# GpSimd makes the clamps of two of seventeen weight pieces; ranks and loads are renumbered

## The chip, the cores and the metric

The kernel runs on one core of a Trainium2 chip. The core has a matrix engine (TensorE, PE in the rows; its weight loads are PEld), a vector engine (VectorE, DVE), an activation engine (ScalarE, ACT), a general engine (GpSimd, POOL) and an engine that issues transfers (SyncE, SP; its queue is SPq). Each works off its own list of instructions in order; semaphores hold an instruction until what it needs is there. The metric is the device time of one execution in microseconds.

## The reference

One attention with product features, followed by a mixer of two small networks, for batches of 4, a sequence of 1088 and a width of 128 (4 heads of 32):

```python
def phi(x):
    a = np.einsum('rd,bhsd->bhsr', S1, x)
    b = np.einsum('rd,bhsd->bhsr', S2, x)
    return np.einsum('bhsi,bhsj->bhsij', a, b).reshape(*x.shape[:-1], r * r)
q_p, k_p = (phi(q), phi(k))
kv = np.einsum('bhsf,bhsd->bhfd', k_p, v)
z = np.sum(k_p, axis=2)
x = num / den            # num = q_p kv, den = q_p z + 1e-06, laid out (B, S, 128)
h = np.maximum(xt @ w_tok1, 0.0) @ w_tok2     # xt: x with S and channels swapped
u = x + h.transpose(0, 2, 1)
h2 = np.maximum(u @ w_ch1, 0.0) @ w_ch2       # 128 -> 1536 -> 128
return (u + h2).astype(np.float32)
```

The four weight matrices come in as 64-bit floats.

## The kernel before

**Weights.** The four matrices (0 to 3: wt1, wt2, wc1, wc2) are cut into seventeen pieces, `w00` to `w32` (matrix, then piece), 256 to 512 columns of 128 partitions. `LOADS` is the order in which SP loads the pieces, and with them the keys, queries and values of batches 0 and 1 (`k0`, `q0a`, `q0b`, `v0`, `k1`, `q1`, `v1`). A 64-bit piece (`doubles`) becomes 32-bit by a chain in `convert` (L373 to L416): `abs` (ACT, L384, tile `c`) and `low` (ACT, L388, tile `tail`), then `clamp` (L391), `shift` (L395, into a PSUM bank) and `merge` (L398), all three on DVE, then `add` (POOL, L405 into `whole`, or L407 in place). Pieces of matrices 2 and 3 at once, and those of 0 and 1 later, are split into a high half (`hi`, ACT, L504) and the remainder (`lo`, POOL, L507), tile `halves`. Batch 0 is mixed with `whole` pieces, everything else with halves.

**Stages of a batch b.** `K` projects keys (L534), copies half of them (ACT, L544), multiplies (DVE, L564, tile `k_p`) and sums with the values (PE, L581); ACT copies the result as `kvz` (L591). `Q` makes the query features: for batch 0 on PE (L672) with copies by ACT (L690, L694, tile `xT`) and products on DVE (L700) or POOL (L697); for the others by row writes and reads through memory (L744 to L760) and products on POOL (L770). `A` is the attention (PE, L790), the division (DVE, L806, L808), the token network (L846 or L852, L886, L968 or L972) and, for batch 0, transposes of x (`u0` to `u2`, L877). `U` is the channel network over spans of 384 columns of all batches: a first-layer group of three matmuls on PE (L1022, into one of three PSUM banks `ps_h`), ACT's `hh` (L1026) and DVE's `hl` (L1029), which frees that bank, and a second-layer group of three matmuls (L1035).

**What sets the order.** The program's order is made on the host by a list planner, `Plan.run` (L222). Each operation has a table of engines with costs (`ways`), what it waits for (`after`, `takes`) and a rank: the length of the chain behind it plus a number of its own from `LEAD`. The planner steps through a clock of its own and issues the ready operation of the highest rank. Operations with `port=True` on DVE, and all of POOL, reserve a common `port` in it. Where PE would idle it puts in filler matmuls (`fill`, L362). What it emits is each engine's list, in order; the chip then only waits for semaphores. A buffer of which there are few (`bufs`: four `c`, four `tail`, three `ps_a`, three `ps_h`) is reused in that order.

Of the kernel before, what the change touches and what calls it, by code (L numbers as in the profile page):

```python
# [65 lines left out]

LEAD = {
    "A0.d1": -168600.0,
    "A0.d2": -1620100.0,
    "A0.t2": -90600.0,  # L70
    "A0.u0": -461300.0,
    "A0.u1": 126500.0,
    "A0.ul00": 26500.0,
    "A1.n1": 207400.0,
    "A1.xT0": -108100.0,
    "A2.h0": -154900.0,
    "A2.n0": 210600.0,
    "A2.w1": -3726400.0,
    "A2.w2": -80800.0,
    "A2.x": -16100.0,  # L80
    "A2.xb": -788400.0,
    "A3.n0": 775400.0,
    "A3.n1": 210300.0,
    "A3.w1": 89200.0,
    "A3.w2": 127600.0,
    "K0.kvz": -2428600.0,
    "K1.c0": 982200.0,
    "K1.kvz": -2006700.0,
    "K1.s": -439400.0,
    "K1.v0": 26700.0,  # L90
    "K1.v4": -1229500.0,
    "K2.p": 5500.0,
    "K2.s": 631300.0,
    "K3.p": 645000.0,
    "Q0.a20": 606400.0,
    "Q0.m20": -56700.0,
    "Q0.p1": 183300.0,
    "Q1.r00": 75800.0,
    "Q1.r01": 221700.0,
    "Q1.r11": -287800.0,  # L100
    "Q3.p": -1564300.0,
    "U0.l": -3600.0,
    "U0.s": -888200.0,
    "U1.ol": 570300.0,
    "U1.s": -310000.0,
    "U10.s": -2000.0,
    "U11.s": -1400.0,
    "U2.f": 181200.0,
    "U2.h": -146700.0,
    "U2.s": -764700.0,  # L110
    "U3.f": 8400.0,
    "U3.s": 5700.0,
    "U4.f": 762600.0,
    "U4.h": 68000.0,
    "U6.s": -230900.0,
    "U8.f": 192500.0,
    "U8.s": -591000.0,
    "U9.f": -390200.0,
    "U9.h": 261700.0,
    "s.low": 6600.0,  # L120
    "s.rows": 95400.0,
    "w00.clamp": -462300.0,
    "w00.lo": -3161100.0,
    "w01.abs": 311700.0,
    "w01.hi": -124600.0,
    "w01.lo": -2636700.0,
    "w02.abs": 28200.0,
    "w02.hi": -455000.0,
    "w02.lo": -4313300.0,
    "w02.low": -1051800.0,  # L130
    "w02.shift": 141200.0,
# [1 line left out]
    "w03.hi": -107500.0,
    "w03.lo": -2645500.0,
    "w03.shift": -1556200.0,
    "w04.hi": -2453000.0,
    "w04.lo": -2852800.0,
    "w10.abs": -1284500.0,
# [1008 lines left out]
```

## Time and profile before

| | us |
|---|---|
| median of 3 runs (220.74 to 222.49) | 220.97 |
| the profiled execution | 220.62 |
| its span, first to last instruction | 218.70 |
| PE busy | 211.2 |
| DVE busy | 137.7 |
| ACT busy | 117.3 |
| POOL busy | 80.3 |

The rows further down are from the profiled execution; times count from the start of its span. A row of the timeline has the start, the duration, the engine, the line, the operation with output and inputs, and in brackets the time for which the engine idled before it and what released it. `x2` after a row means that neighbouring instructions were merged; their durations overlap a little, since an engine begins an instruction before the write of the one before has been acknowledged. Work on engines other than PE costs time only where PE waits for it.

### The profile page before, as it was taken

The numbers are of one execution on the slowest core, as the hardware profiler recorded it, in microseconds if no ns is written. First come the engines' busy times: TensorE is split into PE (matmuls) and PEld (weight loads), VectorE is DVE, ScalarE is ACT, GpSimd is POOL, SyncE is SP. The second block draws the span as 40 slices with busy tenths as digits, with TensorE's granted clock in tenths as the row PEclk, the third lists the DMA queues.
The fourth block names the chain that finished last, engine by engine and source line by source line (L and its number), as shares of the span: only waits on it lengthen the run. The fifth ranks groups of instructions, "written<-read, shape, count | busy, mean of one in ns | idle before, by whom it ended". The sixth has DMA issues, their size and how long they took to land.

```text
span 218.7 us, 4927 instructions
## 1 busy us (share of the span) xinstructions
PE 211.2 (97%) x1884; PEld 199.4 (91%) x1884; DVE 137.7 (63%) x276; ACT 117.3 (54%) x283; POOL 80.3 (37%) x87
## 2 busy tenths in 40 slices
PE   7997999998999999999999999999999999999994
PEld 7766679997998999999999999999999999999993
DVE  2887999879759456555833455568137655556562
ACT  4588799994545324543532544455226544355551
POOL 3165597989899102740500220745003200000000
PEclk9999999999999999999999999999999999999998
DMA  6999996994106589610250258400510000100000
GB/s 194 390 410 407 406 393 205 186 211 151 37 3 226 128 223 155 172 66 3 85 170 0 74 142 146 174 0 27 191 38 1 3 36 0 36 3 36 0 30 27
DMA packets 11399, 28.36 MB, mean 130 GB/s; under 512 B 1520, under 2 KB 5616, under 8 KB 11376
## 3 DMA queue, kind: packets, MB, share of 16 engines
q1 hardware_dynamic: 11232, 27.79, 41.3%
q8 instruction: 15, 0.25, 0.5%
q10 hardware_dynamic: 144, 0.26, 0.4%
q14 instruction: 8, 0.07, 0.1%
HBM read 23.21 MB, written 4.83 MB: 128 GB/s over the span
## 4 chain that ended last, share of the span: by engine, by line
PE 83%; DMA 11%; DVE 1%; SPq 1%; issue 1%; ACT 0%
PE ps_h L1022 33%; PE ps_o L1035 32%; DMA doubles<-wt 11%; PE ps_a L852 4%; PE ps_a L972 4%; PE ps_a L790 3%; PE ps_a L581 3%; PE ps_a L968 1%; PE ps_a L534 1%; SPq L366 1%; PE ps_a L727 1%; DVE k_p L564 1%; PE ps_a L877 0%; PE ps_a L886 0%; DVE hl L1029 0%
## 5 line engine op out<-in xcount | busy, mean ns | idle before, releaser
L1029 DVE SCALAR_TENSOR_TENSOR hl<-ps_h,hh 128x384 fp32r<-128x384 f32 (+2 forms) x144 | 74.9, 532 | 54.9 <-ACT hh L1026 54.5
L1026 ACT ACTIVATE hh<-ps_h 128x384 fp32r<-128x384 f32 (+2 forms) x144 | 67.8, 477 | 58.7 <-PE ps_o L1035 36.2
L1022 PE MATMUL ps_h<-uh,halves 128*128 128x384 f32 (+2 forms) x288 | 88.1, 334 | 0.9 <-DVE hl L1029 0.9
L1035 PE MATMUL ps_o<-hh,halves 128*128 128x384 f32 (+2 forms) x288 | 70.6, 327 | 0.0
L1022 PEld LDWEIGHTS ps_h<-uh,halves 128*128 128x128 f32 x288 | 53.3, 188 | 4.0 <-DVE hl L1029 2.7
L1035 PEld LDWEIGHTS ps_o<-hh,halves 128*128 128x128 f32 x288 | 50.3, 188 | 0.0
L1022 PE MATMUL ps_h<-ul,halves 128*128 128x384 f32 (+2 forms) x144 | 47.0, 327 | 0.0
L1035 PE MATMUL ps_o<-hl,halves 128*128 128x384 f32 (+2 forms) x144 | 47.0, 327 | 0.0
L1022 PEld LDWEIGHTS ps_h<-ul,halves 128*128 128x128 f32 x144 | 27.1, 188 | 0.2
L1035 PEld LDWEIGHTS ps_o<-hl,halves 128*128 128x128 f32 x144 | 27.0, 188 | 0.0
L946 POOL TENSOR_TENSOR ul<-us,uh 128x64 fp32r<-128x64 f32 (+4 forms) x15 | 9.6, 656 | 46.5 <-ACT uh L943 46.3
L770 POOL TENSOR_TENSOR qp<-qp,br 128x544 f32<-128x544 f32 x12 | 16.2, 1367 | 13.2 <-PE ps_o L1035 9.7
L818 POOL TENSOR_TENSOR xl<-x,xh 128x384 fp32r<-128x384 f32 x9 | 8.9, 1014 | 13.5 <-ACT xh L814 8.5
L564 DVE TENSOR_TENSOR k_p<-ps_a,a_sb 128x1024 f32<-128x1024 f32 (+1 forms) x12 | 11.0, 948 | 4.3 <-ACT a_sb L544 4.3
L405 POOL TENSOR_TENSOR whole<-c,tail 128x512 int32<-128x512 int32 (+3 forms) x11 | 11.7, 1071 | 3.3 <-ACT abT L736 2.0
L384 ACT ACTIVATE c<-doubles 128x512 f32<-128x512 f32 (+3 forms) x17 | 10.7, 628 | 3.2 <-DMA doubles<-wt 2.2
L507 POOL TENSOR_TENSOR halves<-whole,halves 128x384 fp32r<-128x384 f32 (+3 forms) x11 | 11.5, 1062 | 0.0
L790 PEld LDWEIGHTS ps_a<-kvz,qp 128*64 128x64 f32 x288 | 8.8, 138 | 2.5 <-ACT kvz L591 1.3
L790 PE MATMUL ps_a<-kvz,qp 128*64 128x66 f32 x288 | 9.5, 224 | 1.4 <-ACT kvz L591 1.1
L388 ACT ACTIVATE tail<-doubles 128x512 int32<-128x512 uint32 (+3 forms) x17 | 10.5, 624 | 0.0
L395 DVE TENSOR_SCALAR ps_h<-c 128x512 int32<-128x512 int32 (+3 forms) x17 | 10.3, 617 | 0.1
L398 DVE SCALAR_TENSOR_TENSOR c<-doubles,ps_h 128x512 int32<-128x512 int32 (+3 forms) x17 | 10.3, 609 | 0.1
(78 smaller groups left out, 229.0 us busy)
## 6 DMA issues: line engine op xcount, KB each, us to landing
qp<-rows SPq DMA_DIRECT2D x6, 544.0 KB
br<-rows SPq DMA_DIRECT2D x12, 272.0 KB
doubles<-wc SPq DMA_DIRECT2D x6, 512.0 KB
v_sb<-v SPq DMA_DIRECT2D x4, 594.0 KB
doubles<-wt SPq DMA_DIRECT2D x4, 512.0 KB
k_sb<-kT SPq DMA_DIRECT2D x3, 576.0 KB
xm<-xb SPq DMA_DIRECT2D x3, 576.0 KB
xT<-xm SPq DMA_DIRECT2D x12, 144.0 KB
```

The source lines that it names most:

```text
L384: nc.scalar.activation(f32(t["c"]), f32(high), AF.Abs)
L388: nc.scalar.activation(t["tail"], low.bitcast(U32), AF.Copy, scale=2.0 ** -29)
L395: nc.vector.tensor_scalar(t["ps"], t["c"], 3, 0x3FFFFFFF, op0=ALU.logical_shift_left, op1=ALU.bitwise_and)
L405: engines[e].tensor_tensor(dst(), t["c"], t["tail"], op=ALU.add)
L507: engines[e].tensor_tensor(halves[w, i][:, 1], f32(whole[w, i] if w < 2 else t["c"]), f32(halves[w, i][:, 0]), op=ALU.subtract)
L564: engines["pool" if on_pool else "dve"].tensor_tensor(t["k_p"][:pn, t0 * H:t1 * H], a.unsqueeze(3).broadcast_to([pn, n, R, R]), t["sb", t0 ...
L770: engines[e].tensor_tensor(qp[:, p, cs], qp[:, p, cs], t["br"][:, p, cs], op=ALU.mult)
L790: nc.tensor.matmul(x_ps[c:c + 64, o:o + 2 * (D + 1)], lhsT=qp[:, p, s0 + c:s0 + c + 64], rhs=kvz_all[b % 2][:, p, :2 * (D + 1)], start=Tru ...
L1022: nc.tensor.matmul(h_ps[:, :cn], lhsT=part(2, at[2][e][0], l, at[2][e][1] * P, P), rhs=r[:, :cn], start=(m == 0), stop=(m == 2))
L1026: nc.scalar.activation(t["hh"][:, :cn], t["h"][:, :cn], AF.Relu)
L1029: nc.vector.scalar_tensor_tensor(t["hl"][:, :cn], t["h"][:, :cn], 0.0, f32(t["hh"][:, :cn]), op0=ALU.max, op1=ALU.subtract)
L1035: nc.tensor.matmul(outs[i][:, :cn], lhsT=part(3, at[3][e][0], l, at[3][e][1] * P, P), rhs=r[:, :cn], start=(e == 0 and m == 0), stop=(e == ...
```

## The change

Two pieces, `w03` and `w15`, have their `clamp` on POOL. The new set `CLAMPS_ON_POOL` names them, and the planner is given a cost for that (141 + 1.6 per column, in its own ns). `LEAD` is exchanged as a whole (95 entries against 102), and `LOADS` is put in another order; nothing else is touched. `m.alt` is read by nothing in the kernel.

```diff
-LOADS = "k0 q0a 00 v0 q0b 01 02 03 04 10 k1 11 12 13 q1 20 32 30 21 v1 31 15 22 14".split()
+LOADS = "00 q0a q0b v0 k0 02 01 03 04 10 k1 q1 12 13 11 20 30 32 31 22 21 14 15 v1".split()
+CLAMPS_ON_POOL = {"w03", "w15"}
 LEAD = {
...
-    "w03.clamp": 120200.0,
-    "w15.clamp": 149200.0,
...
+    "w14.clamp": 147200.0,
...
-        def clamp(_):
-            nc.vector.tensor_scalar(f32(t["c"]), f32(t["c"]), LEAST, MOST, op0=ALU.max, op1=ALU.min)
+        def clamp(e):
+            engines[e].tensor_scalar(f32(t["c"]), f32(t["c"]), LEAST, MOST, op0=ALU.max, op1=ALU.min)
...
-        m = plan.add(name + ".clamp", dve2(n), clamp, [a], (), [c_hold], port=True)
+        m = plan.add(name + ".clamp", {"pool": 141 + 1.6 * n} if name in CLAMPS_ON_POOL else dve2(n), clamp, [a], (), [c_hold], port=True)
+        if not keep:
+            m.alt = [{"pool": 141 + 1.6 * n}]
```

The lists of the engines are new everywhere, though mostly by neighbours that swap. Three places follow. Pieces appear in them as `doubles_` with a running number; the line numbers of the changed kernel are 7 to 9 higher.

ACT, from the abs of w02 (before) and of w01 (now) to the first key sums' copy `kvz` and the copies `xT` of the last queries of batch 0. Before (`doubles_91` is w03, `_92` w04, `_93` w10, `_90` w02):

```order
L384 ACTIVATE c<-doubles_91 128x512
L388 ACTIVATE tail<-doubles_91 128x512
L384 ACTIVATE c<-doubles_92 128x256
L388 ACTIVATE tail<-doubles_92 128x256
L388 ACTIVATE tail<-doubles_93 128x384
L591 COPY kvz_82<-ps_o 64x2x33 x2
L690 COPY xT<-ps_a 128x320
L694 COPY xT<-ps_h 128x320
L690 COPY xT<-ps_a 128x320
L388 ACTIVATE tail<-doubles_90 128x512
L798 ACTIVATE den<-ps_a 128x12
```

Now (`_91` is w03, `_90` w01, `_92` w04, `_93` w10):

```order
L391 ACTIVATE c<-doubles_91 128x512
L395 ACTIVATE tail<-doubles_90 128x512
L391 ACTIVATE c<-doubles_92 128x256
L600 COPY kvz_82<-ps_o 64x2x33 x2
L395 ACTIVATE tail<-doubles_92 128x256
L699 COPY xT<-ps_a 128x320
L703 COPY xT<-ps_h 128x320
L699 COPY xT<-ps_a 128x320
L807 ACTIVATE den<-ps_a 128x12
L395 ACTIVATE tail<-doubles_93 128x384
```

The copy of `kvz` stands behind one tail after the abs of w03 instead of three.

DVE, in the channel network, around the clamps of w14 and w15. Before (`_98` is w32, `_104` w14; the two clamps of 320 columns are w15's and w14's, and fifteen `hl` stand ahead of them in all):

```order
L398 SCALAR_TENSOR_TENSOR c<-doubles_98,ps_h 128x512
L1029 SCALAR_TENSOR_TENSOR hl<-ps_h,hh 128x384 x3
L391 TENSOR_SCALAR c<-c 128x320 x2
L1029 SCALAR_TENSOR_TENSOR hl<-ps_h,hh 128x384 x2
L395 TENSOR_SCALAR ps_h<-c 128x320
L1029 SCALAR_TENSOR_TENSOR hl<-ps_h,hh 128x384
L398 SCALAR_TENSOR_TENSOR c<-doubles_104,ps_h 128x320
L395 TENSOR_SCALAR ps_h<-c 128x320
```

Now (`_99` is w32, `_104` w15, `_103` w14; the clamp is w14's, and seventeen `hl` stand ahead of it):

```order
L405 SCALAR_TENSOR_TENSOR c<-doubles_99,ps_h 128x512
L1038 SCALAR_TENSOR_TENSOR hl<-ps_h,hh 128x384
L402 TENSOR_SCALAR ps_h<-c 128x320
L1038 SCALAR_TENSOR_TENSOR hl<-ps_h,hh 128x384
L405 SCALAR_TENSOR_TENSOR c<-doubles_104,ps_h 128x320
L1038 SCALAR_TENSOR_TENSOR hl<-ps_h,hh 128x384 x4
L398 TENSOR_SCALAR c<-c 128x320
L1038 SCALAR_TENSOR_TENSOR hl<-ps_h,hh 128x384
L402 TENSOR_SCALAR ps_h<-c 128x320
L405 SCALAR_TENSOR_TENSOR c<-doubles_103,ps_h 128x320
```

One clamp has left DVE, the other stands alone and further back, and the shift of w15 stands three `hl` earlier than a shift of 320 columns did.

POOL, from the split of w31 to the last two query products of batch 1 (`qp`). Before (`halves_698` is w31, `_759` w22, `_836` w32, `whole_892` and `_904` w15 and w14; the split of w21 stands just ahead):

```order
L507 TENSOR_TENSOR halves_698<-c,halves_698 128x512
L407 TENSOR_TENSOR c<-c,tail 128x512
L507 TENSOR_TENSOR halves_644<-whole_515,halves_644 128x384
L507 TENSOR_TENSOR halves_759<-c,halves_759 128x512
L770 TENSOR_TENSOR qp<-qp,br 128x544
L407 TENSOR_TENSOR c<-c,tail 128x512
L770 TENSOR_TENSOR qp<-qp,br 128x544
L507 TENSOR_TENSOR halves_836<-c,halves_836 128x512
L1051 TENSOR_TENSOR o_sb<-uh,ul 128x384
L507 TENSOR_TENSOR halves_717<-whole_481,halves_717 128x384
L405 TENSOR_TENSOR whole_892<-c,tail 128x320
L405 TENSOR_TENSOR whole_904<-c,tail 128x320
```

(then the last two products). Now (`halves_713` is w31, `_786` w22, `_836` w32; the splits of w21 and of a 384-wide piece stand just ahead):

```order
L516 TENSOR_TENSOR halves_713<-c,halves_713 128x512
L414 TENSOR_TENSOR c<-c,tail 128x512
L516 TENSOR_TENSOR halves_721<-whole_406,halves_721 128x384
L398 TENSOR_SCALAR c<-c 128x320
L516 TENSOR_TENSOR halves_786<-c,halves_786 128x512
L414 TENSOR_TENSOR c<-c,tail 128x512
L779 TENSOR_TENSOR qp<-qp,br 128x544
L516 TENSOR_TENSOR halves_836<-c,halves_836 128x512
L779 TENSOR_TENSOR qp<-qp,br 128x544
L412 TENSOR_TENSOR whole_884<-c,tail 128x320
L412 TENSOR_TENSOR whole_896<-c,tail 128x320
L516 TENSOR_TENSOR halves_899<-whole_884,halves_899 128x320
```

(then the last two products). The clamp of w15 stands between two splits, the split of w22 behind a further 384-wide one, and one query product has gone behind the split of w32.

## Rows read from the trace of the kernel before

**Rows 1.** the page: busy time of PE, share of the span, instructions

```profile
PE 211.2 (97%) x1884; PEld 199.4 (91%) x1884; DVE 137.7 (63%) x276; ACT 117.3 (54%) x283; POOL 80.3 (37%) x87
```

**Rows 2.** busy by stretch: us, PE, PEld, DVE, ACT, POOL, PEclk, DMA share, GB/s

```profile
60.00:70.00 10.00, 10.00 (x155) 9.15 (x160) 7.48 (x15) 4.92 (x16) 10.00 (x11) 1.00 0.25 81
```

**Rows 3.** waits of PE: line, waited for, total us, times, longest

```profile
PE ps_a L790 <- ACT kvz L591: 1.1, 1, 1.1
```

**Rows 4.** timeline of ACT in the head, around the copy of kvz

```profile
14.72 0.69 ACT L384 ACTIVATE c<-doubles 128x512 f32<-128x512 f32 x1 [0.70 <-DMA doubles<-wt]
15.31 0.67 ACT L388 ACTIVATE tail<-doubles 128x512 int32<-128x512 uint32 x1
15.88 0.41 ACT L384 ACTIVATE c<-doubles 128x256 f32<-128x256 f32 x1
16.21 0.85 ACT L388 ACTIVATE tail<-doubles 128x256 int32<-128x256 uint32 x2
16.96 0.42 ACT L591 COPY kvz<-ps_o 64x66 f32<-64x66 f32 x2
17.41 0.43 ACT L690 COPY xT<-ps_a 128x320 f32<-128x320 f32 x1
```

**Rows 5.** timelines of DVE and PE in the head

```profile
18.27 1.02 DVE L395 TENSOR_SCALAR ps_h<-c 128x256 int32<-128x256 int32 x2
29.18 1.22 DVE L564 TENSOR_TENSOR k_p<-ps_a,a_sb 128x1024 f32<-128x1024 f32 x1
...
30.45 0.55 PE L877 MATMUL ps_a<-ident,x 128*128 128x128 f32 x3 [0.15 <-DVE k_p L564]
...
34.11 2.32 PE L581 MATMUL ps_a<-v_sb,k_p 128*64 128x66 f32 x72
```

**Rows 6.** timeline of SP's queue, issues (start, duration)

```profile
29.05 0.30 SPq L744 DMA_DIRECT2D rows<-abT  x1
30.32 0.30 SPq L744 DMA_DIRECT2D rows<-abT  x1
31.19 0.35 SPq L366 DMA_DIRECT2D k_sb<-kT  x1
```

**Rows 7.** timelines of DVE, POOL and PE around 51 us; one group of clamps

```profile
51.29 1.41 DVE L391 TENSOR_SCALAR c<-c 128x320 f32<-128x320 f32 x1
51.14 1.37 POOL L507 TENSOR_TENSOR halves<-c,halves 128x512 fp32r<-128x512 f32 x1
53.22 0.44 PE L1022 MATMUL ps_h<-uh,halves 128*128 128x384 f32 x1 [0.90 <-DVE hl L1029]
...
L391 DVE TENSOR_SCALAR c<-c 128x384 f32<-128x384 f32 x4 | 1.3, 352 | 0.0
```

**Rows 8.** POOL by form: count, busy us, mean ns, idle before; one timeline row

```profile
L770 POOL TENSOR_TENSOR qp<-qp,br 128x544 f32<-128x544 f32 x12 | 16.2, 1367 | 13.2 <-PE ps_o L1035 9.7 <-DMA br<-rows 3.3 <-POOL ul L946 0.2
L507 POOL TENSOR_TENSOR halves<-c,halves 128x512 fp32r<-128x512 f32 x6 | 8.0, 1340 | 1.5 <-ACT halves L504 1.5
L507 POOL TENSOR_TENSOR halves<-whole,halves 128x384 fp32r<-128x384 f32 x4 | 4.1, 1022 | 0.0
L405 POOL TENSOR_TENSOR whole<-c,tail 128x320 int32<-128x320 int32 x2 | 1.8, 878 | 0.9 <-DVE c L398 0.9
L654 POOL COPY s_spread<-s_blocks 128x256 f32<-128x256 f32 x1 | 0.4, 398 | 2.7 <-DVE s_blocks L403 2.7
L697 POOL TENSOR_TENSOR qp<-xT 128x384 f32<-128x384 f32 x2 | 2.0, 1005 | 6.4 <-ACT xT L690 6.4
...
40.35 2.74 POOL L507 TENSOR_TENSOR halves<-c,halves 128x512 fp32r<-128x512 f32 x2
```

**Rows 9.** timelines of DVE and PE: twelfth hl, first use of w22, attention

```profile
47.28 0.55 DVE L1029 SCALAR_TENSOR_TENSOR hl<-ps_h,hh 128x384 fp32r<-128x384 f32 x1
...
49.03 0.34 PE L1022 MATMUL ps_h<-uh,halves 128*128 128x384 f32 x1
60.65 2.32 PE L790 MATMUL ps_a<-kvz,qp 128*64 128x66 f32 x72
```

More of the change, by code (lines that the diff above doesn't have):

```diff
@@ L65 @@
 KEYS_ON_POOL = set()
+CLAMPS_ON_POOL = {"w03", "w15"}
 LEAD = {
[L68 to L131, printed above, removed]
-    "w03.clamp": 120200.0,
[L133 to L138, printed above, removed]
-    "w10.clamp": 69000.0,
-    "w11.clamp": 246000.0,
-    "w11.hi": -1243300.0,
-    "w11.lo": -134000.0,
-    "w11.low": 448400.0,
-    "w11.merge": -659300.0,
-    "w12.abs": 99900.0,
-    "w12.hi": 475400.0,
@@ L147 @@
-    "w12.low": -24500.0,
-    "w12.merge": -269500.0,
-    "w13.hi": -300400.0,
-    "w13.merge": -144100.0,
-    "w13.shift": -1219700.0,
-    "w14.abs": -2780200.0,
-    "w14.clamp": 192400.0,
-    "w15.abs": -4153500.0,
-    "w15.clamp": 149200.0,
-    "w20.clamp": -574900.0,
-    "w20.low": -1570500.0,
-    "w21.low": 310000.0,
-    "w22.abs": -997600.0,
-    "w22.low": -1298000.0,
-    "w32.abs": -2006300.0,
-    "w32.low": -2863700.0,
+    "A0.d0": -120600.0,
+    "A0.d1": -804800.0,
+    "A0.d2": -1067500.0,
@@ new lines @@
+    "K1.kvz": -1115600.0,
+    "K1.v4": -253500.0,
+    "K2.c0": -235200.0,
+    "K3.p": 764300.0,
+    "K3.s": -896200.0,
+    "Q0.a00": -139800.0,
+    "Q0.a11": 171500.0,
+    "Q0.a20": 586400.0,
+    "Q0.b11": 321100.0,
+    "Q0.p2": -471600.0,
+    "Q1.m00": 189000.0,
+    "Q1.r01": -156700.0,
+    "Q2.p": -401200.0,
+    "Q3.p": -3203400.0,
+    "U0.l": -388200.0,
+    "U0.oh": -343700.0,
+    "U0.s": -489000.0,
+    "U1.s": -2281100.0,
+    "U10.s": -13800.0,
+    "U11.f": -12400.0,
+    "U11.s": -13600.0,
@@ new lines @@
+    "U2.f": -129800.0,
+    "U2.l": -1302400.0,
+    "U2.s": -61100.0,
+    "U3.f": 42700.0,
+    "U4.f": 374000.0,
+    "U4.s": -215500.0,
+    "U5.s": -23800.0,
+    "U6.s": -122100.0,
+    "U7.f": -191700.0,
+    "U7.h": 106300.0,
+    "U7.s": -555000.0,
+    "U8.s": 149000.0,
+    "s.low": 118500.0,
+    "v3": -527800.0,
+    "w00.lo": -3021100.0,
+    "w00.low": 25600.0,
+    "w01.clamp": 96800.0,
+    "w01.hi": -78200.0,
+    "w01.lo": -5573600.0,
+    "w01.low": -177200.0,
+    "w02.lo": -4693900.0,
@@ new lines @@
+    "w03.hi": -155900.0,
+    "w03.lo": -2709800.0,
+    "w03.low": -892100.0,
+    "w04.abs": 215400.0,
+    "w04.clamp": 413100.0,
+    "w04.hi": -1905800.0,
+    "w04.lo": -457000.0,
+    "w04.merge": -398500.0,
+    "w10.abs": -554900.0,
+    "w10.hi": -457500.0,
+    "w10.low": -157100.0,
+    "w12.hi": 30700.0,
+    "w12.merge": -24100.0,
+    "w13.hi": 986800.0,
+    "w13.low": -366600.0,
+    "w13.shift": -540600.0,
+    "w14.abs": -680700.0,
+    "w14.clamp": 147200.0,
+    "w14.lo": -487000.0,
@@ L163 @@
+    "w14.low": 28600.0,
+    "w15.abs": -3843300.0,
+    "w15.shift": 198500.0,
+    "w20.hi": 754000.0,
+    "w20.low": 270500.0,
+    "w22.abs": -73100.0,
+    "w22.low": 70900.0,
+    "w30.low": -524000.0,
+    "w30.shift": -98400.0,
+    "w31.abs": 122900.0,
+    "w31.hi": -378000.0,
+    "w32.abs": -581300.0,
+    "w32.clamp": 184400.0,
+    "w32.lo": 51700.0,
+    "w32.low": -2668600.0,
 }
```

21 lines of the change are left out of this document (added).

## The prediction

> **What bounds the kernel now.** I read the page's busy shares first: TensorE (PE) is busy for 211.2 of 218.7 us [rows 1]. No other engine comes near, so the time is PE's own work plus the moments in which PE has nothing to do. The busy time by stretch says where those lie: from 60 us on PE is full, as in the stretch shown (10.00 of 10.00) [rows 2]. So there are two places to look at: the head, up to about 34 us, in which the weights are converted and batch 0 is mixed, and any hole after it. In the body the change adds no matmul and drops none, and in the head it drops only four filler matmuls, which are the planner's stop-gaps for idle time. Its effect is therefore how much earlier the body starts, plus the holes that close, less the holes that open. PE's waits name two that the change can touch: 1.1 us in the head for the copy of `kvz` by ACT (L591) [rows 3], and one hole of 0.90 us in the body, for an `hl` of DVE (L1029) [rows 7].
>
> **The change, term by term.**
>
> *Head: the copy of kvz.* The head is anchored where piece w03 lands: ACT waits for it and starts at 14.72 [rows 4]. Its landing should not move. Eight loads stand in the queue up to and with 03, before (k0 q0a 00 v0 q0b 01 02 03) and now (00 q0a q0b v0 k0 02 01 03): the same eight. Before, ACT did w03's abs and tail, w04's abs, then two tails (w04, w10), and the copy of kvz at 16.96, the q copies from 17.41. Now, by the order, come w03's abs, w01's tail (as wide as w03's), w04's abs, and kvz; w10's tail goes behind. With the spacings of the rows (0.59, 0.57, 0.33) kvz starts at 14.72 + 1.49 = 16.21. It takes 0.45 (16.96 to 17.41), w04's tail alone some 0.33 (the spacing of its equally wide abs), and the q copies start at 16.99: **0.42 us earlier**.
>
> Does that reach the body? The work behind these copies on DVE is the same pieces in the same places, only with other piece numbers, up to the key product of batch 1 (29.18), which PE waits for at 30.45 [rows 5]. The clamp of w03 leaves DVE, but from a place where DVE waited for ACT anyway, so I count nothing for it. So u1 starts at 30.03, and the value sums of batch 1 (L581), at 34.11 before, want to start at 33.69. These need the values v1, and v1 is now the last of the weights' loads (slot 25 of SP's queue) instead of slot 21. SP issues each load as an older one lands: the issues at 29.05, 30.32 and 31.19 are spaced 1.27 for a 512 KB piece and 0.87 for a 320 KB one [rows 6]. Eight issues lie between an issue and the landing that allows it, so 31.19 is the landing of slot 23. Two loads were left behind it, 512 and 320 KB, so the stream of equal bytes ends at 31.19 + 1.27 + 0.87 = 33.33. That is 0.36 us before v1 is needed. Cost 0, but the cover is thin.
>
> *The hole.* Before, the clamps of w15 and w14 stand together on DVE in front of the sixteenth `hl`. The second takes 1.41 us, where a wider one takes 0.352 in the mean, because GpSimd (POOL) runs a split from 51.14 to 52.51 and the clamp gets through only at its end [rows 7]. The `hl` behind it is late, its PSUM bank with it, and the next first-layer group on PE starts at 53.22 after 0.90 us of idling [rows 7]. Now w15's clamp is POOL's, and w14's stands alone, two `hl` later. It can still be held by a POOL instruction, but look at what waits behind it: the eighteenth `hl`, then the 21st first-layer group, which takes over that bank. Between the 18th group and the 21st, PE's order has two more groups of the first layer and four of the second. A group is three matmuls, 0.52 us as the body's rows are spaced. So PE has 6 x 0.52 = 3.1 us of work there, against one POOL instruction of at most 1.37 [rows 8], the clamp itself (0.35), and one `hl` (0.55). Term: **0.90 us** gained.
>
> Here the Trainium skill speaks against the change. SBUF — State Buffer, "Who interferes with whom", says that GpSimd and a DVE instruction in a 2-port mode take the pair of ports whole, that the one that issues first blocks the other, and that issue order decides; the clamp held for 1.41 us agrees. Read strictly, a clamp on POOL holds the port as a clamp on DVE waits for it, and the hole would only move: the sum would then be 0.42 alone. I go by the order above, in which the wait has cover.
>
> *What POOL pays.* POOL gets two instructions that no row of before shows: a clamp, one input, 128x512 and 128x320. Bounds for 320: from below the one-input copy of 128x256 scaled, 0.398 x 320/256 = 0.50; from above the two-input add, 0.878 [rows 8]. I take 0.6, near the copy, which has one input as well. The w03 clamp runs while POOL waits for q copies: free. The w15 clamp stands in a queue that PE follows closely, so I add it up. Before, the splits of w21 and w31 start at 40.35 [rows 8]; less 0.42 that is 39.93. Then, by the order, two 512 splits and one 384, one 512 add (a split's price), one 384 split, the clamp: 3 x 1.34 + 2 x 1.02 + 0.6 = 6.66, to 46.6. The split of w22 ends at 47.9. PE's row at 49.03 is the first that uses w22 [rows 9]; less 0.42, and two matmuls of 0.17 further for the low half, that is 48.96: in time by 1.0. After it come a 512 add, a product of 544, w32's split, a product, two 320 adds, a 320 split and two products: 47.9 + 2 x 1.34 + 4 x 1.37 + 3 x 0.88 = 58.7. The next attention of PE, at 60.65 before [rows 9], comes at 60.65 - 0.42 - 0.90 = 59.3. In time by 0.6; at the upper price of a clamp by 0.3. Cost 0, bounds 0 and about 0.5 if durations add up without their overlaps.
>
> DVE gets a new wait, the shift of w15 for POOL's clamp. Behind it are further `hl`. POOL's clamp ends at 46.6; DVE comes to this shift after its twelfth `hl`, the one that ran from 47.28 to 47.83 before [rows 9], so to 47.4 now. In time by 0.8.
>
> *Sum.* 0.42 + 0.90 = 1.32. The profiled execution took 220.62 us, of which the span is 218.70 and 1.92 lie around it; 218.70 - 1.32 + 1.92 = **219.3**. The median of the three runs shown, 220.97, is 0.35 above that execution; I predict against the execution. Behind 60 us PE is full, so nothing more is won there, and the tail is the same four groups.
>
> **Rivals.**
> *The likeliest, 219.3:* both terms hold. Its own range is 218.8 to 219.9. Chance 0.45.
> *The hole moves instead of closing, 220.2:* w14's clamp, POOL's clamp of w15 or the attention that waits for POOL's last product costs a wait of the same size; only 0.42 is kept. For it: covers of 0.3 to 0.9 us in a queue that I added up over twenty instructions. Against: the cover of w14's clamp is over 3 us of PE work. Chance 0.26.
> *More than the two terms, 218.6:* the value sums end at 34.11 + 2.32 = 36.4 [rows 5], and to the group at 49.03 PE does 23 groups of 0.52 in 12.6 us, which by themselves are 12.0; so about 0.65 us is lost there in small waits, and another order could close them all: 219.3 - 0.65 = 218.65. For it: these follow a DVE that clamps hold up. Against: no single wait of PE above 0.3 us is named there. Chance 0.14.
> *v1 comes late, up to 221.1, slower than before:* the value sums wait for v1, and PE stands in order behind them. Each us past 33.69 costs one us; from 35.0 on (33.69 + 1.32) the kernel is slower than before. The latest that the stream could end is 35.5, if the row writes mix in; 219.3 + 1.8 = 221.1. For it: a cover of only 0.36. Against: the bytes ahead of v1 are those that had landed at 33.33 before. Chance 0.09.
> *POOL's first clamp pays for loading its code, 219.3 + (x - 2.8):* POOL has never run this operation before w03. w03's abs is ready at 15.4 (14.72 and 0.69 [rows 4]). DVE's shift of w03 is the second of two at 18.27, so it started at about 18.6 before [rows 5], and 0.42 earlier is 18.2. A price x up to 2.8 is free; above that everything in DVE's queue is late, and from x = 4.1 on the kernel is slower than before. Against it: POOL's first two-input product costs no more than the next (mean 1005 ns over both) [rows 8], so x should be near 0. Chance 0.06. GPSIMD Engine Reference of the Trainium skill, "2.1 Instruction dispatch", gives about 6 us for the first call to a freshly loaded kernel; by that figure the time would be an estimated 222.5, and nothing in this trace shows such a load.
>
> **How the numbers follow.** A change of 1% is about what a measurement of this kernel can tell from none; from 220.97 that is 218.8 and 223.2. Faster by over 1% is the third case and a little of the first's lower edge: 0.15. Slower by over 1% needs the code load or something I have not seen: 0.08. The rest, 0.77, is within 1%. The range must leave out two in ten: 218.4 takes in the third case, 221.2 the late v1.
>
> **What would show it.** Right: the copy of kvz starts near 16.2 and the first value sums of batch 1 near 33.7; PE's waits no longer have 0.9 us for `hl`; POOL's 128x320 clamp takes 0.5 to 0.9; the attention stands near 59.3. Wrong: the copy of kvz not earlier, which would mean that w03 landed later; a wait of the value sums (L581) for the load of v1; a wait of DVE's shift for POOL; a wait of the attention for POOL's product; or a first POOL clamp of several us.

## The result, and the profile after

The changed kernel takes 218.28 us (median of six runs, 218.02 to 218.36) against 220.86 us for the kernel before beside it: a ratio of 0.9869, 95% interval 0.9839 to 0.9899. It is 1.3% faster. Two later sets of runs of the same file, each beside the kernel before on another chip, gave 0.9912 (0.9887 to 0.9937; 218.59 us) and 0.9897 (0.9874 to 0.9921; 218.48 us). The forecast was 219.3 us with a range from 218.4: the sign was right, and the forecast gain (1.32 us from the profiled execution) was about half of the measured one (2.40). The first set lies just below the range, the two later sets inside it. One run of a later kernel (220.84 us, w03's clamp alone on POOL) was over 1.5% above that kernel's fastest run and is left out of its figures.

| | before | after | difference |
|---|---|---|---|
| profiled execution, us | 220.62 | 218.22 | -2.40 |
| its span, us | 218.7 | 216.3 | -2.4 |
| copy of kvz by ACT starts | 16.96 | 15.68 | -1.28 |
| value sums of batch 1 on PE start | 34.11 | 33.28 | -0.83 |
| attention of batch 1 on PE starts | 60.65 | 58.80 | -1.85 |

After the change each line number of the kernel is 7 to 9 higher than in the rows of before. The page's busy time of PE (us, share of the span, instructions) against [rows 1]:

```profile
PE 209.9 (97%) x1876; PEld 198.7 (92%) x1876; DVE 136.7 (63%) x274; ACT 117.4 (54%) x284; POOL 83.1 (38%) x88
```

PE's busy time is 1.3 us shorter: four fillers are gone (38 of their records against 46), and some losses that count as busy (below). The waits of PE (line, waited for, total us, times, longest):

```profile
PE ps_o L369 <- POOL ident masks.py:199: 1.4, 1, 1.4
PE ps_a L799 <- ACT kvz L600: 0.4, 1, 0.4
PE ps_a L855 <- DVE x L817: 0.3, 1, 0.3
PE ps_a L895 <- ACT h L873: 0.3, 1, 0.3
PE ps_a L886 <- DVE k_p L573: 0.2, 1, 0.2
```

The 0.9 us for `hl` [rows 7] is gone, and the wait for the copy of `kvz` fell from 1.1 [rows 3] to 0.4. Where the copy comes from, in ACT's timeline (start, duration, line, out<-in), against [rows 4]:

```profile
13.33 0.49 ACT L699 COPY xT<-ps_a 128x384 f32<-128x384 f32 x1
13.69 0.72 ACT L391 ACTIVATE c<-doubles 128x512 f32<-128x512 f32 x1
14.27 0.71 ACT L395 ACTIVATE tail<-doubles 128x512 int32<-128x512 uint32 x1
15.34 0.44 ACT L391 ACTIVATE c<-doubles 128x256 f32<-128x256 f32 x1 [0.36 <-DMA doubles<-wt]
15.68 0.42 ACT L600 COPY kvz<-ps_o 64x66 f32<-64x66 f32 x2
```

w03's abs starts at 13.69, directly behind a copy: the load was there. Before, ACT had stood idle for it until 14.72. Now ACT waits 0.36 us for the next load, w04. POOL's two clamps and DVE's, from the timelines of POOL and DVE:

```profile
15.58 1.91 POOL L398 TENSOR_SCALAR c<-c 128x512 f32<-128x512 f32 x1
45.75 1.28 POOL L398 TENSOR_SCALAR c<-c 128x320 f32<-128x320 f32 x1
50.81 1.30 POOL L516 TENSOR_TENSOR halves<-c,halves 128x512 fp32r<-128x512 f32 x1
...
47.06 0.49 DVE L402 TENSOR_SCALAR ps_h<-c 128x320 int32<-128x320 int32 x1 [0.32 <-POOL c L398]
51.56 0.74 DVE L398 TENSOR_SCALAR c<-c 128x320 f32<-128x320 f32 x1
```

POOL's clamp is dearer than its sum of two inputs of the same width (0.878 for 128x320 in [rows 8]), and DVE's shift of w15 waits 0.32 us for it. w14's clamp on DVE (51.56) is held until POOL's split has ended, 0.74 instead of some 0.3, and no wait of PE follows.

**Where the 2.40 us are.** 0.83 are in the head. The hole of before costs more than its wait says. PE's timeline of before around it; between these rows stands the one at 53.22 in [rows 7]:

```profile
51.98 0.34 PE L1035 MATMUL ps_o<-hl,halves 128*128 128x384 f32 x1
...
53.50 0.34 PE L1022 MATMUL ps_h<-ul,halves 128*128 128x384 f32 x1
```

From 51.98 to 53.22 are 1.24 us where the rows of the body are 0.17 apart, and from 53.22 to 53.50 are 0.28: the hole costs 1.07 + 0.11 = 1.18 us, not 0.90. The wait is counted from the modelled end of the last matmul, 0.34 after its start. Two smaller losses went too, behind the point from which I had called PE full. In before, the query projection of a later batch (L727) stands by itself among the channel network's matmuls; after, value sums and keys follow it directly. PE's timelines of before and then of after at this place:

```profile
69.50 0.31 PE L1035 MATMUL ps_o<-hl,halves 128*128 128x320 f32 x1
69.74 0.69 PE L727 MATMUL ps_a<-q_sb,s_rows 64*32 64x272 f32 x16
70.36 0.41 PE L1022 MATMUL ps_h<-uh,halves 128*128 128x320 f32 x1
70.61 0.31 PE L1022 MATMUL ps_h<-ul,halves 128*128 128x320 f32 x1
```

```profile
68.69 0.69 PE L736 MATMUL ps_a<-q_sb,s_rows 64*32 64x272 f32 x16
69.34 2.32 PE L590 MATMUL ps_a<-v_sb,k_p 128*64 128x66 f32 x72
71.47 1.24 PE L543 MATMUL ps_a<-s_blocks,k_sb 128*64 128x64 f32 x36
```

Rows of one kind are 0.15 apart there; from the last row of the channel network to the projection it is 0.24, and from the first row after it to the next 0.25, so an excursion costs about 0.2. PE's order goes over between matmuls on `halves` and others 25 times before and 23 times after: one excursion fewer. And one pair of matmuls at 89.67 of before lasts 0.78 instead of 0.51, a stall of 0.28 us that after does not have. 0.83 + 1.18 + 0.2 + 0.28 = 2.5, against 2.40 measured. The part behind the attention is not one execution's chance: from the start of the attention of batch 1 to the start of the last matmul PE takes 154.55 us before and 153.93 after; it is 154.5 to 154.7 in the five other profiles with the order of before (the kernel planned anew aside), and 153.9 to 154.2 in the eleven others with the order of after.

### The profile page after: what moved, and what is told of

It reads as the page before. It is cut to its first block, busy times and chain, and to the rows that moved or that the text cites. A ratio compares the mean times of both kernels' runs of the same rounds, so it can differ in the third digit from the quotient of the medians.

```text
span 216.3 us, 4917 instructions
## 1 busy us (share of the span) xinstructions
PE 209.9 (97%) x1876; PEld 198.7 (92%) x1876; DVE 136.7 (63%) x274; ACT 117.4 (54%) x284; POOL 83.1 (38%) x88
## 4 chain that ended last, share of the span: by engine, by line
PE 79%; DVE 5%; ACT 5%; DMA 4%; SPq 2%; issue 2%; POOL 1%; DVEq 0%; POOLq 0%
PE ps_h L1031 32%; PE ps_o L1044 31%; DMA doubles<-wt 4%; PE ps_a L861 4%; PE ps_a L981 4%; PE ps_a L799 3%; PE ps_a L590 2%; SPq L373 2%; ACT halves L513 2%; DVE ps_h L402 2%; ACT hh L1035 1%; DVE c L405 1%; PE ps_a L543 1%; ACT tail L395 1%; DVE x L817 1%
## 5 line engine op out<-in xcount | busy, mean ns | idle before, releaser
L1031 PE MATMUL ps_h<-uh,halves 128*128 128x384 f32 (+2 forms) x288 | 87.1, 332 | 0.0
```

What stands on the lines that cost most here:

```text
L1031: nc.tensor.matmul(h_ps[:, :cn], lhsT=part(2, at[2][e][0], l, at[2][e][1] * P, P), rhs=r[:, :cn], start=(m == 0), stop=(m == 2))
```

## The experiments

Theory 1: the gain is the order (ranks and loads), which takes DVE's held clamps away from an `hl` that PE waits for. Rival: POOL's clamps do it. Theory 2, for the head: the landing of w03 moved. By the trace's landing events fifteen of w03's sixteen parts had landed at 13.52 us before, and the sixteenth at 14.69; at 12.41 a packet of the instruction queue had begun, one in that stretch of 1.05 us. The window's line on that queue (packets, MB, share of the sixteen DMA engines):

```profile
q8 instruction: 1, 0.02, 6.2%
```

6.2% of 1.05 us on sixteen engines is one engine for the whole stretch. After, the packet began at 13.15, and it is w04's last part that is late: 15.32, the others by 13.96. The issue that waits for w03's landing stands at 14.71 before and 13.31 after. Rival: the new order of the loads itself brings w03 earlier.

**The engine alone.** The changed kernel, with both clamps made by DVE in the same places:

```diff
-            engines[e].tensor_scalar(f32(t["c"]), f32(t["c"]), LEAST, MOST, op0=ALU.max, op1=ALU.min)
+            nc.vector.tensor_scalar(f32(t["c"]), f32(t["c"]), LEAST, MOST, op0=ALU.max, op1=ALU.min)
```

> The changed kernel with the same ranks and loads and the same places, but the clamps of w03 and w15 made by DVE where they stand in the planner's order. Theory (the order did it, not the engine): the hole at 53 us stays closed, because w14's and w15's clamps no longer stand together ahead of a due hl; PE names no wait for hl above 0.3 us and the time is within 0.3 us of the changed kernel, 218.0 to 218.6. Rival (POOL's clamps did it): the clamp of w15, back on DVE, is held by a POOL instruction, hl and PE behind it wait again, and 0.5 to 0.9 us are lost: 218.8 to 219.2. In the head, w03's clamp on DVE costs 0 to 0.4 us, since the merge behind it is on the way to the copy of xT.

Measured: 218.31 us, ratio 0.9902 (0.9869 to 0.9934), span 216.0, no wait for `hl` in PE's list. w15's clamp on DVE took 0.32 us and w03's 0.41. The order brings the gain without POOL's clamps. Ranks and loads were not tried apart, so which of the two brings which part is not shown. With w03's clamp on POOL and w15's on DVE:

```diff
+            (nc.gpsimd if name == "w03" else nc.vector).tensor_scalar(f32(t["c"]), f32(t["c"]), LEAST, MOST, ...
```

> The changed kernel with w03's clamp on POOL and w15's back on DVE in its place. POOL's clamp of w15 took 1.28 us in a queue that PE follows with about 0.1 us to spare at the attention near 58.8, and DVE's shift waited 0.32 us for it. Theory (nothing of PE waits for either): within 0.3 us of the changed kernel run beside it. Rival (POOL's 1.28 us delays PE): 0.3 to 0.6 us faster than the changed kernel.

Measured: 218.80 us (median of eleven runs, 217.55 to 220.56), ratio 0.9924 (0.9896 to 0.9953), beside 0.9912 for the changed kernel itself; profiled span 216.2. PE's list of the changed kernel names no wait that ends with POOL's 1.28 us, and by the ratios this kernel is not the faster one, so the rival is not seen. The intervals overlap too far to exclude it. The fastest runs of the two kernels with w15's clamp on DVE (217.48 and 217.55) lie 0.5 us below the fastest of all 18 runs of the changed kernel (218.02): a cost of that size in the best executions stays possible.

**The engine in the old order.** The kernel before, w15's clamp on POOL, nothing else:

```diff
-            nc.vector.tensor_scalar(f32(t["c"]), f32(t["c"]), LEAST, MOST, op0=ALU.max, op1=ALU.min)
+            (nc.gpsimd if name == "w15" else nc.vector).tensor_scalar(f32(t["c"]), ...
```

> The kernel before with one thing changed: the clamp of w15 is made by POOL, in the same place of the planner's order (behind a product, ahead of the split of a 512 piece); ranks and loads stay. Theory (order, not engine): w14's clamp still stands right ahead of the sixteenth hl and is still held by a POOL instruction, which now ends 1.3 us later; the hole at 53 us stays or grows: 220.9 to 221.9. Rival (the engine closes the hole): one clamp fewer ahead of the hl, the hole goes: 219.9 to 220.2.

Measured: 220.45 us, ratio 0.9999 (0.9987 to 1.0012). Both expectations miss the reason. The hole for `hl` did close, but PE then waited for the split that POOL now reached behind a clamp of 1.36 us. DVE's clamp, POOL's clamp and split, and PE in this run's timelines:

```profile
50.32 0.63 DVE L391 TENSOR_SCALAR c<-c 128x320 f32<-128x320 f32 x1
50.73 1.36 POOL L391 TENSOR_SCALAR c<-c 128x320 f32<-128x320 f32 x1
52.06 1.27 POOL L507 TENSOR_TENSOR halves<-c,halves 128x512 fp32r<-128x512 f32 x1
53.38 0.44 PE L1035 MATMUL ps_o<-hh,halves 128*128 128x384 f32 x1 [0.80 <-POOL halves L507]
```

This is the rival of the prediction in which the hole moves, in its pure form. With both clamps on POOL, and the planner left to order all work anew under the old ranks and loads:

```diff
-LOADS = "00 q0a q0b v0 k0 02 01 03 04 10 k1 q1 12 13 11 20 30 32 31 22 21 14 15 v1".split()
+LOADS = "k0 q0a 00 v0 q0b 01 02 03 04 10 k1 11 12 13 q1 20 32 30 21 v1 31 15 22 14".split()
 ...
+# LEAD: that of the kernel before, as a whole
```

> The changed kernel with the ranks and the loads of the kernel before: the planner's rule that puts both clamps on POOL stands alone, and the planner orders the rest anew around it. Theory: the order was tuned to the clamps' places, so by itself the move of two clamps brings nothing or a loss, 220.5 to 223. Rival: the move of the clamps is what brings the gain, 218.5 to 219.5.

Measured: 236.86 us, ratio 1.0747 (1.0683 to 1.0812). PE has 1990 matmul records instead of 1884, and 152 of them are fillers instead of 46: the planner itself foresaw idle time and filled it. So the move of the clamps by itself brings a loss. That the old ranks fit only the old places of the clamps is my reading of it; no run tests it.

**The hole alone.** The kernel before, with w14's clamp emitted behind the seventeenth `hl`:

```diff
         def clamp(_):
-            nc.vector.tensor_scalar(f32(t["c"]), f32(t["c"]), LEAST, MOST, op0=ALU.max, op1=ALU.min)
+            def now():
+                nc.vector.tensor_scalar(f32(t["c"]), f32(t["c"]), LEAST, MOST, op0=ALU.max, op1=ALU.min)
+            if name == "w14":
+                held.append([2, now])      # run behind the second hl from here
+            else:
+                now()
...
```

(the function that emits `hl` counts down and runs it).

> The kernel before with one instruction moved: DVE's clamp of w14 stands behind the seventeenth hl instead of ahead of the sixteenth. Ranks, loads and engines stay. Theory (the hole is this clamp's wait and nothing else ends near it): the hole of 0.9 us at 53 us closes, and the kernel gains 0.9 to 1.1: 219.5 to 219.7. Rival (POOL's queue, which waits for the landing of br near 47, ends next to it): PE then waits for a split of POOL, as it did for 0.8 us where w15's clamp was POOL's, and 0.3 or less is gained: 220.2 to 220.5.

Measured: 219.49 us, ratio 0.9946 (0.9924 to 0.9967): by the medians 0.9 us below the kernel before beside it. DVE and PE in its timelines:

```profile
50.41 1.31 DVE L393 TENSOR_SCALAR c<-c 128x320 f32<-128x320 f32 x1
52.23 0.44 PE L1028 MATMUL ps_h<-uh,halves 128*128 128x384 f32 x1 [0.26 <-DVE hl L1035]
```

One clamp is still ahead of the `hl`, held by a product of POOL, and 0.26 us of the hole are left. In the profiles PE takes 25.92 us from the value sums of batch 1 to its attention, against 26.55 before and 25.52 after the whole change: 0.63 of the 0.98 us by which the span is shorter. The rest is in the head, where w03 was in time in this execution. By the medians, one moved instruction gives a third to a half of what the whole change gave.

**The fillers and the instruction packet.** The trace of before has 15 packets on the instruction queue and 3768 records of PE (matmuls and weight loads). If a packet is fetched about every 250 instructions of PE, an estimate from these two numbers, its moment should follow the number of fillers. In the first kernel six fillers of the changed one became 21 small ones, in the second the fillers were joined, in the third those of the kernel before:

```diff
-                nc.tensor.matmul(spare_ps[:, :P], lhsT=ident, rhs=ident, start=True, stop=True)
+                nc.tensor.matmul(spare_ps[:64, :64], lhsT=ident[:, :64], rhs=ident[:, :64], ...   # 21 for 6
```

```diff
+    wide = const.tile([P, 3 * P], F32, name="wide")
+    nc.gpsimd.memset(wide, 0.0)
 ...
-            for _ in range(n):
-                nc.tensor.matmul(spare_ps[:, :P], lhsT=ident, rhs=ident, start=True, stop=True)
+            for _ in range(n // 3):
+                nc.tensor.matmul(spare_ps[:, :3 * P], lhsT=ident, rhs=wide, start=True, stop=True)
...
```

> The changed kernel with six of its filler matmuls (the two groups of three ahead of 8.8 us) made as 21 small ones of 64x64: 60 more instructions for PE, no more time. Theory A (instruction packet): in the kernel before, a 16 KB packet of the instruction queue started at 12.41 us, took 1.05 us on one of the sixteen DMA engines, and w03's share on that engine came 1.2 us late (ACT's abs of w03 at 14.72); in the changed kernel the packet started at 13.15, behind w03, and hit w04. A packet is fetched about every 250 PE instructions, so 60 more put it at about 11.5 to 12.4: w03 lands late again, its abs starts at 14.4 to 14.7 instead of 13.69, the copy of kvz at about 16.1 instead of 15.68, the value sums of batch 1 near 33.7 instead of 33.28, and the kernel takes about 0.4 us more than the changed one: 218.7. Theory B (the order of the loads alone, k1's late issue above all, brought w03 earlier): nothing moves, abs of w03 at 13.7, 218.3.

> The changed kernel with its filler matmuls joined into ones of 384 columns (a group of seven becomes two, of three one): about 36 fewer instructions for PE ahead of 13 us. Theory A (instruction packet): the packet that started at 13.15 us now starts at about 13.7 and is behind w04 too; ACT's abs of w04, which waited 0.36 us for its load (15.34), starts at 14.98, the copy of kvz at 15.3 instead of 15.68, and the value sums of batch 1 near 32.9 instead of 33.28: about 217.9. Theory B (order of the loads alone): the rows stay, 218.3.

> The kernel before with nothing of the change, only its filler matmuls joined into ones of 384 columns: about 32 fewer instructions for PE ahead of 12.8 us. Theory A (instruction packet): the packet that started at 12.41 us comes at 13.2 to 14.5, behind w03; w03's abs starts at 14.0 (right behind the copies of ACT) instead of 14.72, the copy of kvz at about 16.3 instead of 16.96, and the value sums of batch 1 near 33.4 to 33.5 instead of 34.11; the 0.90 us hole at 53 us stays: about 220.0. Theory B (the order of the loads alone): the rows stay and the time too, 220.9.

Measured: 218.99 us (0.9928, 0.99 to 0.9955), 218.48 (0.9902, 0.987 to 0.9935) and 220.56 (1.0009, 0.9985 to 1.0032). The packet began at 14.11, 16.45 and 12.82: with more instructions (14.11, from 13.15) later, not earlier. So my rule for its moment is wrong, and what sets it stays open. In none of the three was w03 late. The first lost 0.5 us to the fillers themselves (w03's abs at 14.20, all copies ahead of it later; value sums at 33.59); the second had w04 in time and `kvz` at 15.39 as expected, but PE had begun 0.3 us later and the value sums stood at 33.28 all the same. The third is the telling one. ACT in its head, and PE's waits:

```profile
13.79 0.70 ACT L388 ACTIVATE c<-doubles 128x512 f32<-128x512 f32 x1
...
16.25 0.42 ACT L595 COPY kvz<-ps_o 64x66 f32<-64x66 f32 x2
```

```profile
PE ps_h L1026 <- DVE hl L1033: 1.4, 1, 1.4
PE ps_a L794 <- ACT kvz L595: 0.8, 1, 0.8
```

With w03 in time and the fillers joined, the head of the kernel before is 0.7 us earlier (value sums at 33.42), and the hole took it all back: 1.4 us instead of 0.9, the same span. There POOL waited 0.83 us for `br` to land, its product ran from 47.01 as it had from 46.88 before, and the clamps that wait for POOL ended at 52.45. With w14's clamp moved as above and the fillers joined:

> The same move of w14's clamp, and the filler matmuls joined to ones of 384 columns, which brought the copy of kvz and the value sums of batch 1 0.7 us earlier and then lost all of it in the hole (1.4 us instead of 0.9). Theory (head and hole only pay together): with the clamp out of the way the 0.7 us of the head are kept as far as POOL's queue allows, which is held by br's landing: 218.9 to 219.4, earlier than the move alone by 0.3 to 0.7. Rival (POOL's queue is the next bound): no more than the move alone, PE waits 0.5 us or more for a split of POOL.

Measured: 219.38 us, ratio 0.9941 (0.9921 to 0.9961), no better than the move alone (0.9946). In the profiled execution the value sums stood at 33.66, since PE had waited 0.4 us for v0; so the test says nothing on whether head and hole pay together.

**The kernel before, a second profile.**

> The kernel before once more, for its profile. Theory (w03's late landing in its first profile was that execution's chance): the issue that waits for w03's landing stands near 13.5 us instead of 14.71, ACT's abs of w03 near 13.9 to 14.1, the copy of kvz near 16.4, the value sums of batch 1 near 33.7; and since the hole's end hangs on POOL's queue behind the landing of br, the hole is 0.9 to 1.4 us and the span again 218.2 to 218.8. Rival (it belongs to the kernel): 14.7, 16.96 and 34.11 again.

Measured: 221.33 us in one run, span 219.4. w03 is late again. ACT's abs, and PE's waits:

```profile
15.38 0.68 ACT L384 ACTIVATE c<-doubles 128x512 f32<-128x512 f32 x1 [0.79 <-DMA doubles<-wt]
```

```profile
PE ps_o L581 <- DMA v_sb<-v: 0.9, 1, 0.9
PE ps_h L1022 <- DVE hl L1029: 0.9, 1, 0.9
```

Everything from v0 on stood 0.7 us later, and the hole was 0.90 as before. So neither theory holds as put. Of four executions with this head and its own fillers w03 was late in two (14.72 and 15.38 here) and in time in two (13.97 and 14.12 in the kernels with w15's clamp on POOL and w14's moved). Where it was in time, the value sums of batch 1 began at 33.67 and 33.76. In the nine profiles of the changed kernel and of those that differ from it only behind 40 us or in the clamps' engine (most of them below), they began at 32.97 to 33.45, but for one at 34.51; the median is 33.27. Where w03 is in time the new head is then about 0.45 us earlier than the old one. By the landing events a load was held in each of the four, but not always the same one. With the packet at 12.41 and at 13.20 (this profile) the last part of w03 came 1.17 and 1.19 us behind the fifteenth. With the packet at 12.49 and 12.61 it came 0.01 us behind, and it was the next load, w04, whose last part came 0.73 and 0.71 us late.

**POOL's price.** Each of POOL's clamps as two instructions:

```diff
-            engines[e].tensor_scalar(f32(t["c"]), f32(t["c"]), LEAST, MOST, op0=ALU.max, op1=ALU.min)
+            if e == "pool":
+                engines[e].tensor_scalar(f32(t["c"]), f32(t["c"]), LEAST, None, op0=ALU.max)
+                engines[e].tensor_scalar(f32(t["c"]), f32(t["c"]), MOST, None, op0=ALU.min)
...
```

> The changed kernel with each clamp of POOL made as two instructions, the maximum and then the minimum. POOL's clamp took 1.91 us for 128x512 and 1.28 for 128x320, longer than its sum of two inputs (1.28 and 0.88). If the price goes by the arithmetic operations, two in one instruction, each of the two takes about half, 0.9 to 1.0 and 0.6 to 0.7, and the sum stays. If it goes by the elements of an instruction whatever it does, each takes as much as the joint one, 1.9 and 1.28. If an instruction with one operation runs like the copy of 128x256 (0.398), each takes 0.8 and 0.5.

Measured, in POOL's timeline:

```profile
15.58 1.53 POOL L399 TENSOR_SCALAR c<-c 128x512 f32<-128x512 f32 x1
17.19 1.49 POOL L400 TENSOR_SCALAR c<-c 128x512 f32<-128x512 f32 x1
46.67 1.01 POOL L399 TENSOR_SCALAR c<-c 128x320 f32<-128x320 f32 x1
47.77 1.01 POOL L400 TENSOR_SCALAR c<-c 128x320 f32<-128x320 f32 x1
```

None of the three: an instruction with one operation takes 0.79 of one with two. Over the 192 columns between the widths that is 2.6 ns a column for one operation and 3.3 for two, with about 0.2 us on top. One run took 220.01 us, with a span of 218.0: PE waited 1.2 us for `qp` in the head and 0.7 for an `hl`. So POOL's queue hides a clamp of 1.9 us in the head, but not two instructions of 3.1 together.

**Why the same file gives 218.1 and 219.4.** The changed kernel again:

> The changed kernel as it is, once more, beside the next three. Its instruction packet started at 13.15 us in the first profile; in the kernel with DVE's clamps, whose TensorE instructions are the same, it started at 13.76 and missed w04. Theory (the packet's moment is not set by the kernel alone): it starts at another time here, and the copy of kvz follows it: 15.2 to 15.3 if no load that is waited for is hit, 15.7 if w04 is, 16.2 if w03 is; value sums of batch 1 at 32.9 to 33.7. Rival (the moment belongs to the kernel): 13.1 to 13.2 again, kvz at 15.68, value sums at 33.28. The time 218.0 to 218.6.

Measured: 218.59 us, ratio 0.9912 (0.9887 to 0.9937), runs from 218.08 to 219.44, profiled span 217.2. The packet began at 13.53, `kvz` at 15.51, value sums at 33.39. So the packet's moment is not set by the kernel alone, as the theory has it, although `kvz` lies between the values that it names; and the span's 0.9 us are elsewhere. DVE's clamp of w32, POOL's sum of w22 and PE in the first profile and in this one:

```profile
43.13 0.43 DVE L398 TENSOR_SCALAR c<-c 128x512 f32<-128x512 f32 x1
43.20 1.52 POOL L414 TENSOR_TENSOR c<-c,tail 128x512 int32<-128x512 int32 x1
```

```profile
43.32 1.59 DVE L398 TENSOR_SCALAR c<-c 128x512 f32<-128x512 f32 x1
43.33 1.29 POOL L414 TENSOR_TENSOR c<-c,tail 128x512 int32<-128x512 int32 x1
45.43 0.45 PE L1031 MATMUL ps_h<-uh,halves 128*128 128x384 f32 x1 [0.73 <-DVE hl L1038]
```

Both come to the port as POOL's split before ends. Where DVE is 0.07 us ahead it goes through and POOL's sum takes 0.2 longer; where it is 0.01 ahead POOL goes first, the clamp ends only after 1.59 us, and PE waits 0.73 for the `hl` behind it: the same mechanism as the hole at 53 us of before, in another place. In eight profiles this pair stands as in the changed kernel: in seven DVE's record begins 0.03 to 0.07 us ahead and the clamp takes 0.43, and in this one 0.01 ahead. A small memset ahead of the one or the other was to settle the order:

```diff
+                if name == "w22":
+                    nc.gpsimd.memset(gap, 0.0)      # POOL later
```

```diff
+            if name == "w32":
+                nc.vector.memset(gap, 0.0)          # DVE later
```

> The changed kernel with a POOL memset of 128x16 ahead of POOL's sum of w22 (128x512, at 43.2 us), so that DVE's clamp of w32 always asks for the port before it. Theory (the order of these two decides 0.9 us): the clamp takes 0.43, the sum of POOL 1.5, no wait of PE for hl, span 216.0 to 216.4, the runs 217.9 to 218.4 with a narrower spread than the changed kernel's. Rival (the spread has another cause): median and spread as of the changed kernel beside it.

> The changed kernel with a DVE memset of 128x16 ahead of DVE's clamp of w32, so that POOL's sum of w22 asks first. Theory (the order of these two decides 0.9 us): the clamp is held to POOL's end and takes 1.4 to 1.6 us, PE waits 0.7 us for hl near 45.4, span 217.0 to 217.3, the runs 218.9 to 219.4. Rival: no more than 0.1 us from the changed kernel beside it.

> The same memset of POOL, and both clamps of w03 and w15 made by DVE in their places. If POOL's clamps bring nothing and the toss is what is left: as the kernel with the memset alone, 217.7 to 218.3. If POOL's clamp of w15 is worth something by itself: slower than it by 0.3 us or more.

> The changed kernel beside the three. Theory: its executions are of two kinds, near 218.2 where DVE's clamp of w32 comes first and near 219.1 where POOL's sum does, so its median lies between those of the two kernels with a memset, and its spread is the widest. Rival: one kind, 218.0 to 218.6, as narrow as the others.

Measured: 218.51 us (0.9896, 0.9875 to 0.9918), 218.82 (0.9911, 0.988 to 0.9942), 218.59 (0.99, 0.9876 to 0.9923) and 218.48 (0.9897, 0.9874 to 0.9921), with runs from 218.2 to 219.4, 217.9 to 220.1, 218.0 to 219.1 and 218.0 to 219.5. The memset on POOL gave hardly a narrower spread (1.2 us, and 1.4 for the changed kernel beside it), the one on DVE (0.07 us) did not change who came first: its clamp took 0.43. So the toss is not all of the spread. The changed kernel's six runs were five from 218.0 to 218.5 and one of 219.5, and its median lies below those of both memsets, not between them. With the memset on POOL, DVE's clamps and POOL's gave the same time (218.59 and 218.51), which agrees with the engine being without effect. The profiled execution of the first shows another part, in PE's waits:

```profile
PE ps_a L683 <- DMA q_sb<-qT: 1.1, 1, 1.1
```

There the first queries landed late, the value sums of batch 1 began at 34.51, and the span was 217.5 although the clamp went through in 0.43. With six memsets on DVE, 0.78 us together:

> The changed kernel with six DVE memsets of 128x16 ahead of DVE's clamp of w32, 0.4 us in all, so that POOL's sum of w22 surely asks first. Theory (the order of these two is worth 0.7 to 0.9 us): the clamp takes 1.2 to 1.6 us, PE waits for hl near 45, span 216.9 to 217.4, the runs 218.9 to 219.4 at the median, 0.5 to 0.9 above the changed kernel. Rival (a wait there is caught up later): PE's wait shows, but the span is within 0.2 us of 216.3.

Measured: 219.05 us, ratio 0.9912 (0.9881 to 0.9943), span 217.3. DVE's clamp and PE's wait:

```profile
43.94 0.99 DVE L401 TENSOR_SCALAR c<-c 128x512 f32<-128x512 f32 x1
```

```profile
PE ps_h L1034 <- DVE hl L1041: 0.8, 1, 0.8
```

POOL's sum now comes first and PE loses 0.8 us that it does not catch up: span 1.0 above the first profile of the changed kernel. The memsets alone put the clamp back by 0.78 us and POOL's hold adds 0.56 (0.99 instead of 0.43), the value sums stood 0.17 later than in the first profile, and the interval of the ratio overlaps that of the changed kernel, so this run does not separate them. That the toss costs some 0.8 us in an execution rests on the two profiles of the unchanged file.

## Why the prediction was right or wrong

*What bounds the kernel.* Right: PE is busy for 97% before and after, and most of the gain came from the head and from the hole at 53 us (some 0.5 us behind it did not, see below).

*Head, 0.42.* The step that failed here is the anchor, "Its landing should not move". In the profiled pair w03 came 1.4 us earlier (14.71 to 13.31 by the issue behind it), the copy of `kvz` 1.28 instead of 0.75, and the value sums 0.83 instead of 0.42 earlier. The instructions that I counted were right: from w03's abs to `kvz` are 1.99 us after: the 1.49 that I had, a wait of 0.36 for w04, and 0.14 of longer spacings. Over the executions in which w03 was in time, the head gained about 0.45, close to the term; the other 0.4 of the pair are the late part of one load, which had been taken for a fixed point of the kernel. What made w03 late is argued and not shown: in the profiles the late part follows an instruction packet, but it is w03's in two of them and w04's in two others, no run moved the packet at will, and what decides which load is hit stays open.

*From the head to the body.* Right: the 0.83 at the value sums stood at `u1` too (30.45 to 29.62). v1 was in time; its late place in the queue cost nothing, and that rival fell.

*Hole, 0.90.* The mechanism was right, and shown by moving w14's clamp alone (0.9 us by the medians, 0.63 at this place in the profile). The size was not: the wait in the list is counted from the modelled end of the last matmul, so the hole was worth 1.18. The Trainium skill, SBUF — State Buffer, "Who interferes with whom", says that issue order decides which of the two engines blocks the other; the two profiles of one file with 0.43 and 1.59 us for the same clamp agree as far as their times resolve it, since DVE's record begins first in both, by 0.07 and by 0.01 us. Its strict reading, that the hole would only move, fits the old order with w15's clamp on POOL (0.80 us of PE's wait for POOL's split in place of 0.90 for `hl`), and not the new one.

*"Behind 60 us PE is full, so nothing more is won there".* The second step that failed, wrong by about 0.5, a term put at nothing: one excursion between kinds of matmul fewer (0.2) and a stall of 0.28 less. A busy share of 10.00 in 10.00 [rows 2] does not show them, since they lie inside the busy time of rows.

*POOL's price.* Wrong: 1.28 us for 128x320, above the upper bound of 0.878 that I took from the sum of two inputs, and 1.91 for 128x512. DVE's shift of w15, said to be in time by 0.8, waited 0.32, and the attention, said to have 0.6 of cover, came at 58.80 behind a product of POOL that ended about 0.1 earlier. PE's list names no wait for any of it, and the kernels with DVE's clamps are not faster by their ratios (0.9902 and 0.99); a cost in the best executions is not excluded (above). No price for a first call is seen: 1.91 and 1.28 differ by a factor of 1.49, their widths by 1.6.

*The sum.* 0.42 + 0.90 = 1.32 against 2.40: 0.41 from the head's anchor, 0.28 from the hole's size and 0.48 from the body, 0.1 more than the difference. The rival "more than the two terms" named 218.6 for small waits ahead of 49 us; the gain was larger and elsewhere.

## What to carry to other kernels

Price a hole by the distance between the starts of the matmuls around it, less their usual spacing, and add the restart; the listed wait is smaller. Before an early DMA wait is used as an anchor, look at the landings of the load's parts: here fifteen of sixteen were there 1.17 us before the last, and the load came 1.4 us earlier in the other kernel. A second profile of the same file would not have told it, since w03 was late in that one too; kernels that differ only further behind had it in time. Where DVE and POOL meet at the shared port, see to it that what is held has work ahead of it that nobody waits for: moving one clamp behind two `hl` was worth 0.9 us by the medians, moving one to the other engine nothing (ratio 0.9999).

## What the runs showed of the hardware that I had not expected

- POOL's clamp with two operations took 1.91 us for 128x512, its sum of two inputs 1.28 to 1.55; a clamp with one operation 1.5. Here a clamp of one input is not cheaper than a sum of two, although the one-input copy of 128x256 took only 0.398 [rows 8].
- One of a load's sixteen parts can come late by itself: in the profile of before the last part of w03 came 1.17 us behind the fifteenth, and the last parts of the next three loads 1.21 behind theirs.
- The same DVE clamp took 0.43 or 1.59 us in two executions of one file, with less than 0.1 us between the starts of the two engines' instructions in both.
